# A third kind of expert tile, weight loads moved to ScalarE's queue, and two smaller moves, in a fused sliding-window attention and mixture-of-experts kernel

## The chip, the cores and the metric

The kernel runs on one core of a Trainium2 chip. The metric is the device time of one execution in microseconds. A core has TensorE (PE: matmuls and transposes, with PEld for its weight loads), VectorE (DVE), ScalarE (ACT), GpSimd (POOL) and SyncE (SP, which here only issues transfers). Each takes its own instructions in order. PE writes to PSUM, which has eight banks of 512 float32 values for each of 128 partitions.

## The reference

Attention first: 8 batches, 8 heads, 576 positions, head size 64; each position sees itself and the 63 before it. The result, as 4608 tokens of 512 values, goes through a mixture of experts: eight experts, each token goes to the one with the largest logit, and the expert's output is weighted with that softmax value.

```python
scores = scale * np.matmul(q, k.transpose(0, 1, 3, 2))
rel = pos[:, None] - pos[None, :]
mask = (rel >= 0) & (rel < window)          # window = 64
attn = softmax(where(mask, scores, -1e9))
x = (attn @ v) as (4608, 512)               # tokens
logits = x @ w_gate                         # (4608, 8)
expert_idx = np.argmax(logits, axis=1)
gate_w = softmax(logits)[its own expert]
for e in range(8):                          # the tokens of expert e
    h = np.maximum(x_e @ w1[e], 0.0)        # w1[e]: 512 x 1024
    y_e = h @ w2[e]                         # w2[e]: 1024 x 512
out = gate_w * y
```

All is float32. The experts have no capacity limit: how many tokens an expert gets is known only on the chip.

## The kernel before

**Attention (to about 217 us).** The 16 pairs of (two batches, two heads) are "units"; each unit is done in three steps of three query tiles, 48 steps in all. `step(s)` (line 941) runs several stages of neighbouring steps: q and k are loaded by SP (`load_qk`, line 537; the last 64 positions by `load_rests`, line 548; v by `load_v`, line 561, which POOL then copies into a second alignment), transposed by PE (line 595), multiplied to scores in banks 0 and 1 (line 628), masked by DVE (line 641), exponentiated by ACT (line 651), transposed (line 659), multiplied with v (`weighted`, line 665, always into bank 6), divided by DVE (`divided`, line 680) and turned for the gate's logits. The order of all instructions is written out by hand (`manual_schedule`): each engine gets them as the code calls them. At the start, all loads stand in SP's queue: q and k of unit 0, the rests of batch group 0, v of unit 0, then q and k of unit 1, and so on (lines 921 to 928).

**Routing (about 217 to 250 us).** Tokens are counted per expert (`choose`, line 733), `starts` (line 216) turns counts into numbers of tiles on DVE, and `slot_table` (line 835) makes the list `perm_i` of the token in each slot. The first two tiles, of expert 0, are computed meanwhile.

**Expert tiles (from about 220 us).** A tile has 256 slots. For a *whole* tile `hidden` (line 336) and `output` (line 393) compute each of the two layers by a Strassen-like scheme with seven products instead of eight of half-size blocks. The weights stand in PE in the first layer, and sums of weight blocks are made by POOL beforehand (`sums_w1`, `sums_w2`). The first layer's seven products go to banks 0, 1 and 6 and end in ACT's relu steps; in the second layer DVE makes sums of the hidden blocks first. An expert's *last* tile with at most 160 tokens is a *half* tile (`half_tile`, line 436): 32 matmuls with standing weights and 160 moving columns, then the second layer with the hidden values standing and the weights moving, for tokens 128 to 159 in four column groups of 32 (line 465), and for the first 128 tokens whole (line 470).

Around each tile (`body`, line 479) the work for others is placed: `finish` (DVE) and `scatter` (POOL) write the tile before; `between` lets POOL form the next weights' sums; `turned_blocks` lets DVE turn the next tile's tokens by 16 block transposes (line 315); `keep_turned` (ACT, line 325) copies them to where PE reads, and `sums_x` (DVE) makes the sums; `gather` (POOL) fetches the tokens of the tile after. The weights have two buffers; those of expert e+1 are loaded by SP at the start of expert e (lines 1066 to 1068), when the buffer of e-1 is free.

Which tiles an expert has is decided on the chip: `expert` (line 1063) emits, for each expert and each possible number of tiles up to three, both kinds of tile as separate code, and each engine branches (lines 1076 and 1077) on registers that hold the number of tiles and of whole tiles.

Of the kernel before, what the change touches and what calls it, by code (L numbers as in the profile page):

```python
# [36 lines left out]
def kernel(  # L37
# [34 lines left out]
    NW = 2  # L72
    QD = 32
    HALF = P + QD
    NCUT = NT // P
    assert D == WINDOW and 2 * D == P and NG * P == DM and NB * WINDOW == S
    assert S - SM == WINDOW and KB == NV + 1 and NTB * P == BG * S and B % BG == 0 and NTILE * TB <= 128 * P
# [13 lines left out]
    info_i = consts.tile([P, 2 * E + 1], I32, name="info_i")  # L91
    fulls_i, all_i, most_i = info_i[:, 0:E], info_i[:, E : 2 * E], info_i[:, 2 * E :]

    places_i = consts.tile([P, E + 1], I32, name="places_i")
    perm_e = consts.tile([P, NE * C], I32, name="perm_e")
# [57 lines left out]
    def sums_w2(e):  # L153
        form(right_sums(G, s2s[e % NW], *w2q(e)))

    def load_w1(e):
        return nc.sync.dma_start(out=w1s[e % NW][:], in_=w1v[e])

    def load_w2(e):
        nc.sync.dma_start(out=w2s[e % NW][:], in_=w2v[e])  # L160


    oh_all = consts.tile([P, E, NJ], BF16, name="oh_all")
# [63 lines left out]
    zrow = consts.tile([1, DM], F32, name="zrow")  # L227
    nc.vector.memset(zrow[:], 0.0)
# [39 lines left out]
    def form_all(parts):  # L268
        for _ in parts:
            pass  # L270
# [205 lines left out]
            keep_turned()  # L476
            sums_x([xn[:, c] for c in range(C)])

    def body(e, last, after, full, between=None, next_x=True):
# [6 lines left out]
        if not full:  # L486
            half_tile(e, blocks, after, next_x)
            return
        form_all(hidden(e, blocks))
        parts = output(e, blocks, next_x)  # L490
        next(parts)
        if after is not None:
            gather(perm_i[:, after])
        form_all(parts)

    with tc.manual_schedule(), ExitStack() as held, ExitStack() as brief:
# [40 lines left out]
        def load_qk(u):  # L537
            bg, g = units[u]
            qks[u] = [qk_m(((u % 3 + 2) % 3 * 2 + n) * 1024, BG, NV, 2, D) for n in range(2)]
            for i in range(BG):  # L540
                for t, src in zip(qks[u], (q, k)):
                    for h in range(2):
                        nc.sync.dma_start(
                            out=t[:, i, :, h, :],
                            in_=src[bg * BG + i, 2 * g + h, 0:SM, :].rearrange("(p j) d -> p j d", j=NV),
                        )

        def load_rests(bg):

            at = 6144 + bg % 2 * 2048  # L550
            vr = qk_m(at + 1024, BG, H, D)
            rests[bg] = [qk_m(at, H, D), qk_m(at + 512, H, D), vr]
            for t, src in zip(rests[bg], (q, k)):
                for i in range(BG):
                    nc.sync.dma_start(
                        out=t[i * D : (i + 1) * D], in_=src[bg * BG + i, :, SM:S, :].rearrange("h p d -> p h d")
                    )
            for i in range(BG):
                nc.sync.dma_start(out=vr[D:P, i], in_=v[bg * BG + i, :, SM:S, :].rearrange("h p d -> p h d"))
# [105 lines left out]
        def weighted(s, pTs):  # L665
            u, c = divmod(s, NST)
            bg, g = units[u]
            va, vb = v_ring[u % NVR]
            px = banks[6](0, 2, ST, VW)
            for m in range(ST):  # L670
                for a, (bp, i) in enumerate(blocks_of(c * ST + m)):
                    vt = va[:, bp, i // 2] if i % 2 or i == 0 else vb[:, bp, i // 2 - 1]
                    for h in range(2):
                        nc.tensor.matmul(  # L674
                            px[a * D : (a + 1) * D, h, m, :], lhsT=pTs[h][:, m, a * D : (a + 1) * D],
                            rhs=vt[:, h, :], start=True, stop=True, skip_group_check=True,
                        )
            return px
# [189 lines left out]

        def loads():

            _, n = nc.values_load_multi_w_load_instructions(info_i[0:1, :], min_val=0, max_val=NT // P)
# [4 lines left out]
            return [(n[e], n[E + e], places[e]) for e in range(E)], places[E], n[2 * E]  # L876

        def after(s, routing, bg):

# [174 lines left out]
    with tc.manual_schedule():  # L1054
        load_w1(1)
        load_w2(1)
        def at(n):
            n = nc.s_assert_within(
                n, 0, NTILE - 1, skip_runtime_bounds_check_because="a tile with a token is one of the NTILE"
            )  # L1060
            return lambda ahead: bass.ds((n + ahead) * C, C)

        def expert(e):

            fulls, tiles, first = regs[e]
            if 0 < e < E - 1:
                load_w1(e + 1)
                load_w2(e + 1)

            def one(n, full, between=None):  # L1070
                slots = at(first + n)
                body(e, slots(0), slots(3), full, between)

            def more(n, between=None):

                with tc.If(tiles > n) as some_left:  # L1076
                    with tc.If(fulls > n, preferred_fallthrough_block=False) as full:
                        one(n, True, between)
                        if n + 1 < KT:
                            more(n + 1)  # L1080
                    with full.Else():
                        one(n, False, between)
                if between is not None:
                    with some_left.Else():
                        between()

            if e:
                one(0, True, partial(sums_w2, e))
            more(1 if e else NE, partial(sums_w1, e + 1) if e + 1 < E else None)

        def any_number():
# [27 lines left out]
                finish()  # L1119
                scatter(perm_i[:, slots(1)])  # L1120

        with tc.If(most < KT + 1) as few:  # L1122
            for e in range(E):
                expert(e)
            finish()
# [33 lines left out]
```

## Time and profile before

| | us |
|---|---|
| median of 3 runs | 714.86 (714.1 to 715.29) |
| profiled execution | 717.81 |
| its span, first to last instruction | 716.0 |
| PE busy | 688.8 (96%) |
| DVE, ACT, POOL busy | 505.5, 259.4, 356.6 |
| granted clock of PE, mean | 0.994 |
| a whole tile (484.40 to 509.00) | 24.6 |
| a half tile (509.00 to 526.70) | 17.7 |

Durations below come from the profiled execution; times are counted from its first instruction. A row of the timeline is start, duration, engine, line of the code, operation, what it writes from what it reads, partitions x elements, how many in a row, and in brackets how long the engine had been idle and what ended that. A row of the waits is who waited for whom, microseconds in all, how often, and the longest. A row of a line's instructions has the least, median and largest duration in ns. PEldq is PE's sequencer, which handles branches and semaphores ahead of the array. PE's durations overlap, so the spacing of starts is what counts.

### The profile page before, as it was taken

What the parts mean: (1) busy time and instruction counts of PE and PEld (TensorE: products, weight loads), DVE (VectorE), ACT (ScalarE), POOL (GpSimd) and SP (SyncE); (2) the same over time, 40 slices, a digit from 0 to 9 for tenths busy, and PEclk for the clock granted to TensorE, in tenths of its full rate; (3) what the DMA queues carried; (4) which work ended last, traced back from release to release, by engine and by line L of the source; (5) the groups of instructions that cost most, each with busy time, mean ns of one, the idle gap of its engine ahead of it and who ended that gap; (6) DMA issues with size and microseconds to landing.
All of it is one profiled execution on the core that took longest, in us unless ns stands there. A gap on an engine that the chain in (4) does not pass through costs nothing. (4 is left out here: it accounts for less than half of the span.)

```text
span 716.0 us, 17981 instructions
## 1 busy us (share of the span) xinstructions
PE 688.8 (96%) x6882; PEld 606.6 (85%) x6882; DVE 505.5 (71%) x1656; ACT 259.4 (36%) x655; POOL 356.6 (50%) x368
## 2 busy tenths in 40 slices
PE   5999999999879999999999999999999999999996
PEld 4787888878768898797999999899979799979995
DVE  3666898898965858685866676586667586667764
ACT  4787888888844211121211121121111121011211
POOL 6113748569375025947562257356264756264022
PEclk9999999999989999999999999999999999999999
DMA  9998889988251382715311531351181531111011
GB/s 165 206 200 184 183 179 229 211 197 235 97 187 38 126 294 66 275 63 190 107 48 61 150 143 61 118 203 37 60 275 60 173 116 57 60 38 45 17 61 58
DMA packets 137143, 94.42 MB, mean 132 GB/s; under 512 B 116591, under 2 KB 116607, under 8 KB 137024
## 3 DMA queue, kind: packets, MB, share of 16 engines
q1 hardware_dynamic: 127328, 62.14, 33.0%
q0 software_dynamic: 9120, 28.60, 12.4%
q10 hardware_dynamic: 576, 2.10, 0.9%
q8 instruction: 74, 1.21, 0.7%
q14 instruction: 45, 0.37, 0.2%
HBM read 73.94 MB, written 20.45 MB: 132 GB/s over the span
## 5 line engine op out<-in xcount | busy, mean ns | idle before, releaser
L315 DVE STREAM_TRANSPOSE v_m<-qk_m 32x256 f32<-32x256 f32 x320 | 139.2, 435 | 8.4 <-DMA qk_m<-x_dram,at_g 2.4
L275 POOL DMA_INDIRECT qk_m<-x_dram,at_g x42 | 45.4, 1081 | 174.8 <-DVE v_m L315 145.8
L344 PE MATMUL bank<-qk_m,s 128*128 128x128 f32 x1024 | 122.5, 275 | 0.4 <-DVE qk_m L365 0.4
L344 PEld LDWEIGHTS bank<-qk_m,s 128*128 128x128 f32 x1024 | 118.3, 192 | 0.6 <-issue 0.6
L651 ACT ACTIVATE pr<-pr,mx 128x128 f32<-128x128 f32 x288 | 89.7, 391 | 33.8 <-DVE mx L641 32.1
L344 PE MATMUL bank<-qk_m,w 128*128 128x128 f32 x768 | 93.9, 275 | 0.8 <-PEq L1076 0.8
L344 PEld LDWEIGHTS bank<-qk_m,w 128*128 128x128 f32 x768 | 90.6, 192 | 4.3 <-issue 3.9
L641 DVE CUSTOM_DVE_ANT_0 pr<-bank,mask 128x128 f32<-128x128 f32 x288 | 64.4, 286 | 29.4 <-PE bank L628 28.0
L384 DVE TENSOR_TENSOR v_m<-bank,v_m 128x256 f32<-128x256 f32 (+1 forms) x95 | 43.8, 480 | 40.9 <-PE bank L388 25.9
L295 POOL DMA_INDIRECT out_dram<-v_m,at_s x42 | 42.6, 1013 | 54.0 <-DVE v_m L384 49.9
L569 POOL COPY v_m<-v_m 64x520 f32<-64x520 f32 x32 | 19.8, 618 | 69.4 <-DMA v_m<-in_v_dram 63.3
L140 POOL TENSOR_TENSOR s<-w 128x1024 f32<-128x1024 f32 x22 | 52.2, 2371 | 0.0
L674 PEld LDWEIGHTS bank<-v_m,pT 128*64 128x64 f32 x1152 | 40.6, 139 | 11.0 <-DVE xs L688 4.9
L674 PE MATMUL bank<-v_m,pT 128*64 128x65 f32 x1152 | 47.3, 229 | 2.2 <-DVE xs L688 2.1
L351 ACT COPY qk_m<-bank 128x512 f32<-128x512 f32 x16 | 9.4, 586 | 108.5 <-PE bank L344 70.3
L388 PE MATMUL bank<-qkT_m,v_m 128*128 128x256 f32 x216 | 48.3, 379 | 0.0
L628 PE MATMUL bank<-qkT_m 64*64 64x128 f32 x1152 | 45.9, 289 | 0.1
L595 PE MATMUL bank<-ident,qk_m 128*128 128x128 f32 x256 | 37.0, 287 | 9.4 <-DMA qk_m<-in_q_dram 7.4
L388 PEld LDWEIGHTS bank<-qkT_m,v_m 128*128 128x128 f32 x216 | 41.0, 190 | 5.5
L327 ACT COPY qk_m<-v_m 128x512 f32<-128x512 f32 x40 | 22.7, 615 | 62.4 <-DVE v_m L315 62.4
L444 PEld LDWEIGHTS bank<-qk_m,w 128*128 128x128 f32 x320 | 43.9, 190 | 0.9 <-issue 0.7
L444 PE MATMUL bank<-qk_m,w 128*128 128x160 f32 x320 | 44.4, 299 | 0.4 <-ACT qk_m L327 0.4
(176 smaller groups left out, 1255.4 us busy)
## 6 DMA issues: line engine op xcount, KB each, us to landing
w<-in_moe_w_dram SPq DMA_DIRECT2D x11, 2048.0 KB, 10.0
qk_m<-in_q_dram SPq DMA_DIRECT2D x72, 128.0 KB, 3.7
qk_m<-in_k_dram SPq DMA_DIRECT2D x72, 128.0 KB, 3.8
v_m<-in_v_dram SPq DMA_DIRECT2D x64, 128.0 KB, 3.9
qk_m<-in_moe_w_dram SPq DMA_DIRECT2D x3, 2048.0 KB, 11.1
x_dram<-xs POOLq DMA_DIRECT2D x6, 512.0 KB
x_dram<-xs POOLq DMA_DIRECT2D x3, 768.0 KB
w<-in_moe_w_dram ACTq DMA_DIRECT2D x4, 512.0 KB, 5.8
```

The lines of the kernel that those rows point to most:

```text
L140: op()
L275: G.indirect_dma_start(out=xg[c], out_offset=None, in_=x_dram[:, :], in_offset=bass.IndirectOffsetOnAxis(ap=at_g[:, c : c + 1], axis=0),)
L295: put = G.indirect_dma_start(out=out[:, :], out_offset=bass.IndirectOffsetOnAxis(ap=at_s[:, c : c + 1], axis=0), in_=ys[c], in_offset=None ...
L315: V.transpose(out=xn[b * QD : (b + 1) * QD, :, :, a * QD : (a + 1) * QD].rearrange("p c g i -> p (c g) i"), in_=rows[a * QD : (a + 1) * QD ...
L344: nc.tensor.matmul(acc[:, f, :], lhsT=a[:, g, f * P : (f + 1) * P], rhs=b[:, g, :], start=(first and f == 0 and g == 0), stop=(g == HG - 1 ...
L384: plus = lambda out, a, b: V.tensor_tensor(out=out, in0=a, in1=b, op=ALU.add)
L388: nc.tensor.matmul(acc, lhsT=a[:, f, :], rhs=b[:, f, :], start=(start and f == 0), stop=(stop and f == HF - 1), skip_group_check=True,)
L444: nc.tensor.matmul(acc[:, i], lhsT=w1[:, g, f * P : (f + 1) * P], rhs=xq[:, g].rearrange("p c s -> p (c s)")[:, 0:HALF], start=(i + g == 0 ...
L628: nc.tensor.matmul(out_, lhsT=qT[rows, t, a * WINDOW : (a + 1) * WINDOW], rhs=rhs, start=True, stop=True, skip_group_check=True,)
L641: V.tensor_tensor_reduce(out=prs[h][:, m, :], in0=scs[h][:, m, :], in1=mask[:, m0 + m, :], scale=-scale, scalar=-2 * MASKED, op0=ALU.add, ...
L651: nc.scalar.activation(out=y, in_=y, func=AF.Exp, scale=-1.0, bias=mx[:, h, m : m + 1])
L674: nc.tensor.matmul(px[a * D : (a + 1) * D, h, m, :], lhsT=pTs[h][:, m, a * D : (a + 1) * D], rhs=vt[:, h, :], start=True, stop=True, skip_ ...
```

## The change

1. *A third kind of tile.* A last tile with at most 96 tokens is a *rest* tile (`rest_tile`): in both layers the tokens stand and the weights move. Tokens 64 to 95 use four column groups of 32, tokens 0 to 63 two groups of 64. The hidden values then have tokens on the partitions, so PE transposes them before the second layer. `starts` now makes one number for each expert, the sum of three counts of tiles, with limits of 0, 96 and 160 tokens for the last tile, and the branches compare it with 3n, 3n+2 and 3n+1.
2. *The next expert's weights* are issued on ACT's queue in the expert's first tile, after the third and the fifth of the seven first-layer products, not by SP at the start of the expert.
3. *The last two steps' values* (`weighted`) go to banks 0 and 1, not to bank 6.
4. *The first k* (unit 0's, and the rest of batch group 0) are issued by ACT, and q and k of unit 1 stand before v of unit 0.

```diff
+    REST = P - QD
-    fulls_i, all_i, most_i = info_i[:, 0:E], info_i[:, E : 2 * E], info_i[:, 2 * E :]
+    kinds_i, most_i = info_i[:, 0:E], info_i[:, E:]
+    parts_i = consts.tile([P, 2, E], I32, name="parts_i")
-    def load_w1(e):
-        return nc.sync.dma_start(out=w1s[e % NW][:], in_=w1v[e])
+    def load_w1(e, queue=nc.sync):
+        queue.dma_start(out=w1s[e % NW][:], in_=w1v[e])
...
     def starts():
-        for got, slots in ((fulls_i, TB - 1 - HALF), (all_i, TB - 1)):
-            V.tensor_scalar(out=got, in0=count[:], scalar1=float(slots), scalar2=float(TB), op0=ALU.add, op1=ALU.max)
+        def tiles_over(got, rest):
+            V.tensor_scalar(
+                out=got, in0=count[:], scalar1=float(TB - 1 - rest), scalar2=float(TB), op0=ALU.add, op1=ALU.max
+            )
             V.tensor_single_scalar(got, got, TB.bit_length() - 1, op=ALU.arith_shift_right)
-        V.tensor_copy(out=nt[:], in_=all_i)
-        V.tensor_reduce(out=most_i, in_=nt[:], axis=AX.X, op=ALU.max)
+        tiles_over(kinds_i, 0)
+        V.tensor_copy(out=nt[:], in_=kinds_i)
...
+        for n, rest in enumerate((REST, HALF)):
+            tiles_over(parts_i[:, n], rest)
+            V.tensor_tensor(out=kinds_i, in0=kinds_i, in1=parts_i[:, n], op=ALU.add)
+        V.tensor_copy(out=e_m[:], in_=kinds_i)
+        V.tensor_reduce(out=most_i, in_=e_m[:], axis=AX.X, op=ALU.max)
...
+    L = P // 2
+    hr, hr4 = qk_m(8192, FF // 2), qk_m(8192 + FF // 2, FF // 4)
+    ht, ht4 = qk_m(8960, HF, 2, L), qk_m(8960 + HF * P, HF // 2, 4, QD)
+    def rest_tile(e, blocks, after, next_x):
+        w1, w2 = w1s[e % NW], w2s[e % NW]
+        def rows(acc, tokens, ways):
+            n, width = P // ways, FF // ways
+            for g in range(NG):
+                for c in range(ways):
+                    nc.tensor.matmul(
+                        acc[c * n : (c + 1) * n, 0:width], lhsT=xq[:, g, 0, tokens],
+                        rhs=w1[:, g, c * width : (c + 1) * width], start=(g == 0), stop=(g == NG - 1),
+                        skip_group_check=True,
+                    )
+        a, b = banks[0](0, FF // 2), banks[1](0, FF // 4)
+        rows(b, slice(L, L + QD), 4)
+        relu(out=hr4, in_=b)
+        rows(a, slice(0, L), 2)
+        relu(out=hr, in_=a)
+        for h, t, acc in ((hr4, ht4, banks[3](0, HF // 2, P)), (hr, ht, banks[6](0, HF, P))):
+            for i in range(h.shape[1] // P):
+                nc.tensor.transpose(out=acc[:, i], in_=h[:, i * P : (i + 1) * P], identity=ident[:])
+            nc.scalar.copy(out=t.rearrange("p i c s -> p i (c s)"), in_=acc)
+        V.memset(v1, 0.0)
+        V.memset(yw2, 0.0)
+        form_all(blocks)
+        if after is not None:
+            gather(perm_i[:, after])
+        y, y4 = banks[7](0, DM), y2(0, P)
+        for f in range(FT):
+            for c in range(4):
+                nc.tensor.matmul(
+                    y4[c * QD : (c + 1) * QD], lhsT=ht4[:, f % (HF // 2), f // (HF // 2)],
+                    rhs=w2[:, f, c * P : (c + 1) * P], start=(f == 0), stop=(f == FT - 1), skip_group_check=True,
+                )
+        for f in range(FT):
+            for c in range(2):
+                nc.tensor.matmul(
+                    y[c * L : (c + 1) * L, c * HM : (c + 1) * HM], lhsT=ht[:, f % HF, f // HF],
+                    rhs=w2[:, f, c * HM : (c + 1) * HM], start=(f == 0), stop=(f == FT - 1), skip_group_check=True,
+                )
+        for c in range(4):
+            nc.scalar.copy(out=yps[0][L : L + QD, c * P : (c + 1) * P], in_=y4[c * QD : (c + 1) * QD])
+        if next_x:
+            keep_turned()
+            sums_x([xn[:, c] for c in range(C)])
+        nc.scalar.copy(out=yps[0][0:L, hi_], in_=y[L:, hi_])
+        V.tensor_copy(out=yps[0][0:L, lo_], in_=y[0:L, lo_])
...
-        form_all(hidden(e, blocks))
+        for n, _ in enumerate(hidden(e, blocks), 1):
+            if n in loads:
+                loads[n]()
...
-                for t, src in zip(qks[u], (q, k)):
+                for t, src, queue in zip(qks[u], (q, k), (nc.sync, nc.sync if u else nc.scalar)):
...
-            px = banks[6](0, 2, ST, VW)
+            px = banks[6 if s < N - 2 else s - N + 2](0, 2, ST, VW)
...
+        load_qk(1)
         load_v(0)
-        load_qk(1)
...
             if 0 < e < E - 1:
-                load_w1(e + 1)
-                load_w2(e + 1)
+                loads = {3: partial(load_w1, e + 1, nc.scalar), 5: partial(load_w2, e + 1, nc.scalar)}
...
-                with tc.If(tiles > n) as some_left:
-                    with tc.If(fulls > n, preferred_fallthrough_block=False) as full:
-                        one(n, True, between)
+                with tc.If(kind > 3 * n) as some_left:
+                    with tc.If(kind > 3 * n + 2, preferred_fallthrough_block=False) as full:
+                        one(n, whole_tile, between)
                         if n + 1 < KT:
                             more(n + 1)
                     with full.Else():
-                        one(n, False, between)
+                        with tc.If(kind > 3 * n + 1) as half:
+                            one(n, half_tile, between)
+                        with half.Else():
+                            one(n, rest_tile, between)
```

More of the change, by code (lines that the diff above doesn't have):

```diff
@@ L90 @@
     perm_i = consts.tile([P, NS], I32, name="perm_i")
-    info_i = consts.tile([P, 2 * E + 1], I32, name="info_i")
-    fulls_i, all_i, most_i = info_i[:, 0:E], info_i[:, E : 2 * E], info_i[:, 2 * E :]
+    info_i = consts.tile([P, E + 1], I32, name="info_i")
+    kinds_i, most_i = info_i[:, 0:E], info_i[:, E:]
+    parts_i = consts.tile([P, 2, E], I32, name="parts_i")
     places_i = consts.tile([P, E + 1], I32, name="places_i")
@@ L154, in sums_w2, with load_w2 @@
         form(right_sums(G, s2s[e % NW], *w2q(e)))
-    def load_w1(e):
-        return nc.sync.dma_start(out=w1s[e % NW][:], in_=w1v[e])
-    def load_w2(e):
-        nc.sync.dma_start(out=w2s[e % NW][:], in_=w2v[e])
+    def load_w1(e, queue=nc.sync):
+        queue.dma_start(out=w1s[e % NW][:], in_=w1v[e])
+    def load_w2(e, queue=nc.sync):
+        queue.dma_start(out=w2s[e % NW][:], in_=w2v[e])
     oh_all = consts.tile([P, E, NJ], BF16, name="oh_all")
@@ L477, in half_tile @@
             sums_x([xn[:, c] for c in range(C)])
-    def body(e, last, after, full, between=None, next_x=True):
+    L = P // 2
[46 more added lines that the diff above has]
+        V.tensor_copy(out=yps[0][0:L, lo_], in_=y[0:L, lo_])
@@ L481, in body, with whole_tile @@
+    def whole_tile():
+        pass
+    def body(e, last, after, tile_, between=None, next_x=True, loads=()):
         finish()
@@ L485, in body @@
         blocks = turned_blocks() if next_x else iter(())
-        if not full:
-            half_tile(e, blocks, after, next_x)
+        if tile_ is not whole_tile:
+            tile_(e, blocks, after, next_x)
             return
-        form_all(hidden(e, blocks))
+        for n, _ in enumerate(hidden(e, blocks), 1):
+            if n in loads:
+                loads[n]()
         parts = output(e, blocks, next_x)
@@ L540, in load_qk @@
             for i in range(BG):
-                for t, src in zip(qks[u], (q, k)):
+                for t, src, queue in zip(qks[u], (q, k), (nc.sync, nc.sync if u else nc.scalar)):
                     for h in range(2):
-                        nc.sync.dma_start(
+                        queue.dma_start(
                             out=t[:, i, :, h, :],
@@ L552, in load_rests @@
             rests[bg] = [qk_m(at, H, D), qk_m(at + 512, H, D), vr]
-            for t, src in zip(rests[bg], (q, k)):
+            for t, src, queue in zip(rests[bg], (q, k), (nc.sync, nc.sync if bg else nc.scalar)):
                 for i in range(BG):
-                    nc.sync.dma_start(
+                    queue.dma_start(
                         out=t[i * D : (i + 1) * D], in_=src[bg * BG + i, :, SM:S, :].rearrange("h p d -> p h d")
@@ L869, in loads @@
         def loads():
-            _, n = nc.values_load_multi_w_load_instructions(info_i[0:1, :], min_val=0, max_val=NT // P)
+            _, n = nc.values_load_multi_w_load_instructions(info_i[0:1, :], min_val=0, max_val=3 * NT // P)
             _, places = nc.values_load_multi_w_load_instructions(
@@ L875, in loads @@
             )
-            return [(n[e], n[E + e], places[e]) for e in range(E)], places[E], n[2 * E]
+            return list(zip(n[0:E], places[0:E])), places[E], n[E]
         def after(s, routing, bg):
@@ L1063, in expert, with one @@
         def expert(e):
-            fulls, tiles, first = regs[e]
+            kind, first = regs[e]
+            loads = {}
             if 0 < e < E - 1:
-                load_w1(e + 1)
-                load_w2(e + 1)
-            def one(n, full, between=None):
+                loads = {3: partial(load_w1, e + 1, nc.scalar), 5: partial(load_w2, e + 1, nc.scalar)}
+            def one(n, tile_, between=None):
                 slots = at(first + n)
-                body(e, slots(0), slots(3), full, between)
+                body(e, slots(0), slots(3), tile_, between, loads=() if n else loads)
             def more(n, between=None):
-                with tc.If(tiles > n) as some_left:
-                    with tc.If(fulls > n, preferred_fallthrough_block=False) as full:
-                        one(n, True, between)
+                with tc.If(kind > 3 * n) as some_left:
+                    with tc.If(kind > 3 * n + 2, preferred_fallthrough_block=False) as full:
+                        one(n, whole_tile, between)
                         if n + 1 < KT:
@@ L1087, in expert @@
             if e:
-                one(0, True, partial(sums_w2, e))
+                one(0, whole_tile, partial(sums_w2, e))
             more(1 if e else NE, partial(sums_w1, e + 1) if e + 1 < E else None)
@@ L1120, in any_number @@
                 scatter(perm_i[:, slots(1)])
-        with tc.If(most < KT + 1) as few:
+        with tc.If(most < 3 * KT + 1) as few:
             for e in range(E):
```

## The prediction

> **What bounds the kernel now.** I read the page's busy shares first, then who TensorE (PE) waited for, then the two kinds of expert tile in order of time, and last PE's branches.
>
> ```profile
> PE 688.8 (96%) x6882; PEld 606.6 (85%) x6882; DVE 505.5 (71%) x1656; ACT 259.4 (36%) x655; POOL 356.6 (50%) x368
> ```
> ```profile
> PE bank L595 <- DMA qk_m<-in_q_dram: 7.4, 4, 4.7
> PE bank L699 <- DVE pT L661: 3.1, 4, 1.4
> PE bank L914 <- DVE hi_e L907: 2.7, 1, 2.7
> PE bank L674 <- DVE xs L688: 2.1, 4, 0.9
> PE bank L595 <- DMA qk_m<-in_k_dram: 1.8, 4, 0.7
> PE bank L344 <- PEq L1076: 0.8, 1, 0.8
> PE bank L344 <- DVE qk_m L365: 0.4, 1, 0.4
> ```
> ```profile
> 509.05 8.86 PE L444 MATMUL bank<-qk_m,w 128*128 128x160 f32 x64
> 517.83 1.96 PE L465 MATMUL bank<-qk_m 128*32 128x128 f32 x64
> 519.72 7.13 PE L470 MATMUL bank<-qk_m 128*128 128x512 f32 x16
> 526.69 0.50 PE L344 MATMUL bank<-qk_m,w 128*128 128x128 f32 x3
> ```
> ```profile
> 457.11 1.89 PE L388 MATMUL bank<-w,v_m 128*128 128x256 f32 x8
> 459.79 2.02 PE L344 MATMUL bank<-qk_m,w 128*128 128x128 f32 x16 [0.78 <-PEq L1076]
> ```
> ```profile
> L1077 PEldq COMPARE_BRANCH  x19: 67/342/6568, 270.9 to 705.7; - x19
> ...
> L1076 PEldq COMPARE_BRANCH  x2: 190/2218/4245, 455.0 to 459.4; - x2
> ```
> PE is busy 96% and its waits sum to some 21 us, most of them before 20 us and between 200 and 220 us. The expert stage is a line of tiles without gaps: a whole tile takes 24.6 us (484.45 to 509.05), a half tile 17.65 us (509.05 to 526.69), whatever VectorE (DVE) and ScalarE (ACT) do beside it. So a microsecond taken from or added to PE in this stage moves the end by as much. The last two fences show the only thing that stopped PE between tiles: a branch that took 4245 ns instead of the usual 68 to 342.
>
> **Part 1, the rest tile.** From the inputs I worked out the routing: 669, 400, 748, 505, 592, 390, 566, 738 tokens. Expert 0's count stays over 512. The last tiles hold 157, 144, 236, 249, 80, 134, 54 and 226 tokens, so five are half tiles now (L444: 320 records, 64 a tile) and two of them, of experts 4 and 6, become rest tiles. A float32 matmul shows as two records. Start to start, a record costs 111.6 ns for 128 moving columns, 138 ns for 160 (8.78/64), 216 for 256 and 436 for 512 (6.97/16), and 29.5 ns for 128 columns in four 32-wide column groups (1.89/64), a quarter. The rest tile issues:
> - 32 tokens, four groups, 256 columns: 32 records at 216/3.8 = 57 ns: 1.8 us.
> - 64 tokens, two groups, 512 columns: 16 at 436/2: 3.5 us. No row has exactly two groups; the nearest is L674 (64-wide outputs, 65 columns), 24 records in 0.90 us = 37 ns, against some 59 for one alone by the same slope. I take 2 and bound it by 1.
> - 6 transposes, 12 records at 110 to 128 ns (L306): 1.4 us. Those of the second half wait for the relu of 512 columns (0.6 us, L454) that starts as PE ends the 512-column products; the first half's four records hide 0.5 us of it: gap 0.45.
> - second layer: 64 records at 29.5 = 1.9 us, and 32 of 256 columns in two groups at 108 = 3.5 us.
>
> The sum is 12.5 us, against 17.65: -5.15 a tile, -10.3 in all. DVE must do finish, two memsets and 16 block transposes (16 x 0.44) first, about 8.5 us from the tile's start, then ACT's four small copies and keep_turned end near 11.6: under PE's 12.5, cover 0.9 us. The gather leaves at 8.5 and is read some 4 us into the next, whole, tile.
>
> [...] The rest tile changes mode more often than the half tile. The row: L444 to L465 to L470 passes with starts 8.78 and 1.89 us apart and no gap that the trace shows, so I charge nothing; at 0.2 us (estimate: the pipeline tail, 1.96-1.89 and 7.13-6.97) for four more changes it would be 0.8 us a tile, kept for the range.
>
> **Part 2, the branches, which speak against it.** In the program each level has half, full (next level inside), rest, in this order; rest lies behind full. In instructions (four a float32 matmul): half 291, full 337, rest 314. [...] the instruction queue has 74 packets, 1.21 MB, 16.4 KB each; PE's jumps over one half tile took 342 to 348 ns, except 3805 where two block bounds lay between; over 632 instructions 4245; over 960, 6568 and 6132. The 3805 showed as no wait, the two 6 us ones neither, because PE had the 16 long L470 matmuls (7 us) queued. Behind a whole tile the queue holds about 18 records of 216 ns, 3.9 us; behind a rest tile 18 of 108 ns, 1.95 us. I took the block bounds from the jumps of before, and laid the new program on them:
> - expert 2's last full tile must now jump over 632 instructions (before: none): +0.3. Expert 3's second tile now crosses two bounds: +0.3.
> - end of expert 3: the 4.25 us fetch is there already (0.78 exposed), but it lands in a stub behind which another jump follows at once, into a block whose fetch has only begun. In the trace the next fetch starts 0.7 us after the jump, takes 1.0 and is usable 1.4 later: 3.1 us. So 4.25+3.1+0.3-3.9 = 3.7 exposed: +2.9.
> - start of both rest tiles: behind half and full, 628 instructions, a fetch each: +0.5 each. End of expert 4's rest tile: two bounds, 4.1-1.95: +2.2. End of expert 6's: one bound, its block fetched: 0.
> - ends of the halves of experts 0, 1, 5: fetches under the 7 us: 0. Expert 7: +0.1 on a doubtful bound.
>
> Sum +6.8. By the branch row alone[...] (342 ns, hidden by the queue), it would be 0. I take the sum[...].
>
> **Part 3, first k by ScalarE.** SP issues a q or k load of 128 KB in 0.65 us, so its first 26 end at 18.4 us. Six go to ACT, whose six issues (3.9 us) and table load (1.28) end at 6.0, while its first copy is due at about 6.5: covered by 0.5 us. All that SP issues comes 3.9 us sooner, less 2.6 for v(0), which queues behind unit 1's eight (5.2 us): v(0) is issued from 11.2 instead of 10.3 and used at 21.2 before. Early packets arrive at 200 GB/s, SP's pace, and later stretches reach 240, so two queues gain a little: first q and k both at 5.5 (q was at 4.7, k at 6.1), second pair at 7.7. The first scores start at 9.7, not 10.46: -0.75. Then the waits for q at 17.69 (1.07) and at 55.48 and 56.63 (1.13, 0.53) should shrink, as SP issued without a pause from 34 to 75 us and is now 3.9 ahead. All would be -3.5; I take -2.5, since other waits can move up; from 0 to -4.
>
> **Part 4, banks, weights, counts.** The last two values got their own banks: the waits of 0.50 at 213.04 and 0.89 at 216.38 for DVE's division go, but pT's copies end only 0.6 before the second: -1.1. Products x and y take banks 0 and 1 later than their divisions end.
> The next weights leave SP (issued at 284.36 and 292.97, across a gather) for ACT, after the third and fifth product: 0.37 us each, ahead of relu steps with 1.1 us of idle time, so hidden; without cover 0.7 us a tile on the second layer's operands. 4 MB at some 250 GB/s land by 24 us of the tile; POOL's sums need w1 at 25. Gain: the 0.45 wait at 304.05 (L365): -0.45.
> starts() has 14 instead of 9 small DVE operations, at 0.16: 0.8 us, in a stretch (226 to 245) where DVE is full and PE already waits for hi (0.3 at 241.95): +0.8. The 17 registers become 9: nothing that the trace shows.
>
> **Sum.** -10.3 + 6.8 - 2.5 - 1.1 - 0.45 + 0.8 = -6.75. The profiled execution took 717.81 (span 716.0), 2.95 over the median of 714.86; no term depends on that, so 717.81-6.75 is 711.06 as a profiled time and 714.86-6.75 = 708.1 as a median.
>
> **Rivals.**
> - *Fetches cost nothing* [...]: 714.86-10.3-2.5-1.1-0.45+0.8 = 701.3. For it: of PE's six branches of 2.9 us or more, one shows as a wait. Against: that one, 0.78 at 459.79.
> - *The start gives nothing*, as 16 DMA engines are already busy (share 1.00 from 6 to 12 us): 710.6. For it: DMA reads 9 in the slices up to 150 us.
> - *Pairs of 64-wide groups do not overlap*: rows() of 64 tokens and its second layer cost 7.0 instead of 3.5 us each, +7.0 a tile: 708.1+14.0 = 722, slower. It decides from an overlap of 1.35 down, where 3.4 a tile use up the 6.75. Against: 37 ns at L674.
> - *No tile takes the new path*: then -10.3 and +2.2+1.0 of it go, 715.2: ruled out as far as the counts above are right.
>
> **How the numbers follow.** Case one (708.1, own range 704.5 to 711.5) 0.55; fetches free 0.2; start without gain 0.17; pairs 0.05; no new path 0.03. A measurement of this kernel tells about 0.2% (1.4 us) from no change. Slower than 716.3: pairs, and a little of the last, 0.06; within 0.2%: 0.04; faster 0.9. The range reaches to the free fetches, 701, and up to 712.5, where the start gains nothing and mode changes cost 0.8 a tile.
>
> **What would show it.** Right: two rest tiles of about 12.5 us, each behind a gap of about 0.5 us put down to PE's queue; a gap of about 2 us at expert 4's end and 3.5 at expert 3's; first scores before 10 us; no wait at L674's last two groups; 1 us of wait for hi. Wrong: those gaps missing (then near 701), or 64-token groups with over 300 ns a record at 512 columns.

## The result and the profile after

The changed kernel takes **707.78 us** (median of 4 runs, 706.77 to 708.33), the kernel before took 715.08 on the same chip (4 runs, 714.1 to 716.48): a ratio of 0.9884, 95% interval 0.9861 to 0.9906, so 7.3 us less. The profiled execution of after took 708.33 with a span of 706.5; that of before 717.81 and 716.0, which is 2.7 above the median of its kernel. The spans therefore differ by 9.5, and it is these 9.5 that the rows below add up to. The forecast of 708.1 was met, in part by luck: two terms of it, the branches and the start, were wrong in opposite directions.

The busy shares, and who TensorE (PE) waited for in the whole span:

```profile
PE 678.2 (96%) x6894; PEld 594.9 (84%) x6894; DVE 502.8 (71%) x1657; ACT 262.4 (37%) x665; POOL 356.4 (50%) x368
```
```profile
PE bank L664 <- DMA qk_m<-in_q_dram: 6.8, 2, 6.2
PE bank L354 <- issue: 6.2, 4, 3.1
PE bank L983 <- DVE hi_e L976: 2.7, 1, 2.7
PE bank L768 <- DVE pT L730: 1.4, 1, 1.4
...
PE bank L514 <- ACT qk_m L511: 0.7, 2, 0.3
PE bank L501 <- issue: 0.7, 2, 0.3
PE bank L398 <- ACT v_m L412: 0.5, 1, 0.5
```

(Columns: total us, number of waits, longest. L664 is before's L595, L354 its L344, L398 its L388, L983 its L914.) The waits for k are gone and those for q are the first load and one more. One of the signs named ahead fails in this execution: its first scores start at 10.62, not before 10 us (10.46 in before); in the five variants of the changed kernel below that keep its start and its buffers, they start between 9.0 and 9.6. New is 6.2 us in which PE, at the first layer of a whole tile, "waits for issue", that is, for nothing but its own instructions. The 0.45 for the operands of a new expert (L365 before) is gone; there is one new wait of 0.5 for ScalarE in the first tile.

The timeline of PE around expert 4's rest tile (start, us, engine, line, shape, records, and in brackets the idle time ahead):

```profile
509.07 5.52 PE L501 MATMUL bank<-w,qk_m 128*32 128x256 f32 x48 [0.32 <-issue]
514.52 0.44 PE L514 MATMUL bank<-ident,qk_m 128*128 128x128 f32 x2
515.28 0.66 PE L514 MATMUL bank<-ident,qk_m 128*128 128x128 f32 x4 [0.33 <-ACT qk_m L511]
515.87 1.96 PE L525 MATMUL bank<-qk_m 128*32 128x128 f32 x64
517.75 3.67 PE L531 MATMUL bank<-qk_m 128*64 128x256 f32 x32
521.36 0.82 PE L354 MATMUL bank<-qk_m,w 128*128 128x128 f32 x5
```

509.07 to 521.36 is 12.29 us; the other rest tile, 613.38 to 625.67, takes the same. The only idle time inside is the 0.33 ahead of the second transposes.

The end of expert 3, after its last whole tile:

```profile
449.49 1.89 PE L398 MATMUL bank<-w,v_m 128*128 128x256 f32 x8
454.50 0.46 PE L354 MATMUL bank<-qk_m,w 128*128 128x128 f32 x2 [3.13 <-issue]
457.54 3.15 PE L354 MATMUL bank<-qk_m,w 128*128 128x128 f32 x14 [2.58 <-issue]
460.48 2.65 PE L354 MATMUL bank<-qk_m,s 128*128 128x128 f32 x16
462.97 1.95 PE L354 MATMUL bank<-qk_m,w 128*128 128x128 f32 x16
```
```profile
L1146 PEldq COMPARE_BRANCH  x2: 2767/3360/3952, 447.3 to 451.6; - x2
L1146 PEldq EVENT_SEMAPHORE  x1: 51/51/51, 451.4 to 451.4; - x1
```

This is the largest surprise of the profile. PE stops for 3.13 us, issues two records, stops for 2.58 again, and then runs at half speed: 16 records of L354 take 2.65 us in place of 1.95. The clock's record agrees: half rate is granted from 455.1 for 6.8 us. Before, the end of the last whole tile (459.01) to the end of the next expert's first one (484.45) took 25.4 us; now (451.38 to 483.99) it takes 32.6. The second fence shows PE's sequencer there (shortest, median and longest duration in ns, first and last start): a jump of 3952 ns from 447.3, one of 2767 from 451.6, and between them, at 451.4, an instruction on a semaphore. That instruction turns out to matter.

### The profile page after: what moved, and what is told of

Read it like the earlier page. It is cut to its first block, busy times and chain, and to the rows that moved or that the text cites. A ratio compares the mean times of both kernels' runs of the same rounds, so it can differ in the third digit from the quotient of the medians.

```text
span 706.5 us, 18016 instructions
## 1 busy us (share of the span) xinstructions
PE 678.2 (96%) x6894; PEld 594.9 (84%) x6894; DVE 502.8 (71%) x1657; ACT 262.4 (37%) x665; POOL 356.4 (50%) x368
## 3 DMA queue, kind: packets, MB, share of 16 engines
q0 software_dynamic: 9120, 28.60, 12.4%
## 5 line engine op out<-in xcount | busy, mean ns | idle before, releaser
L354 PE MATMUL bank<-qk_m,s 128*128 128x128 f32 x1024 | 123.2, 276 | 0.0
L354 PEld LDWEIGHTS bank<-qk_m,s 128*128 128x128 f32 x1024 | 119.1, 193 | 0.5 <-issue 0.5
L354 PE MATMUL bank<-qk_m,w 128*128 128x128 f32 x768 | 95.8, 278 | 6.2 <-issue 6.2
L354 PEld LDWEIGHTS bank<-qk_m,w 128*128 128x128 f32 x768 | 91.8, 194 | 9.4 <-issue 9.0
L743 PEld LDWEIGHTS bank<-v_m,pT 128*64 128x64 f32 x1152 | 40.6, 139 | 10.2 <-issue 4.3
L398 PE MATMUL bank<-qkT_m,v_m 128*128 128x256 f32 x216 | 48.3, 379 | 0.0
L364 DVE TENSOR_TENSOR qk_m<-bank,qk_m 128x512 f32<-128x512 f32 x16 | 11.1, 691 | 48.6 <-PE bank L354 48.6
L398 PEld LDWEIGHTS bank<-qkT_m,v_m 128*128 128x128 f32 x216 | 41.0, 190 | 5.5
L728 PE MATMUL bank<-ident,pr 128*128 128x128 f32 x288 | 43.3, 288 | 0.0
L664 PE MATMUL bank<-ident,qk_m 128*128 128x128 f32 x256 | 35.8, 286 | 6.8 <-DMA qk_m<-in_q_dram 6.8
## 6 DMA issues: line engine op xcount, KB each, us to landing
qk_m<-in_moe_w_dram ACTq DMA_DIRECT2D x3, 2048.0 KB, 10.2
```

What stands on the lines that cost most here:

```text
L354: nc.tensor.matmul(acc[:, f, :], lhsT=a[:, g, f * P : (f + 1) * P], rhs=b[:, g, :], start=(first and f == 0 and g == 0), stop=(g == HG - 1 ...
L398: nc.tensor.matmul(acc, lhsT=a[:, f, :], rhs=b[:, f, :], start=(start and f == 0), stop=(stop and f == HF - 1), skip_group_check=True,)
L728: nc.tensor.transpose(out=tr[:, m, :], in_=prs[h][:, m, :], identity=ident[:])
L743: nc.tensor.matmul(px[a * D : (a + 1) * D, h, m, :], lhsT=pTs[h][:, m, a * D : (a + 1) * D], rhs=vt[:, h, :], start=True, stop=True, skip_ ...
```

## The experiments

Each ratio is to the kernel before, run beside it on the same chip; the chips differ, so that before's median was 716.3 to 716.8 in these. Against it, the changed kernel's 0.9884 would be 708.0 to 708.5.

### Where PE's code lies: two dead paddings

PE's code is fetched in pieces. In before's trace, from the transfer that starts at 20.24 us up to the one at 217.82, a stretch in which PE takes no branch, there are 26 transfers of 16 KB on an instruction queue (q8) and 6629 records of PE's instructions: 255 for each transfer. The layouts here take blocks of 256 instructions, which agrees with this count.

```
             with half.Else():
                 one(n, rest_tile, between)
+                if e == 0:
+                    for i in range(51):
+                        nc.tensor.matmul(yps[0], lhsT=hp[:, i % FT, 0:P], rhs=w2s[0][:, i % FT, :], ...)
```

(30 in the second kernel.)

> The changed kernel with 51 more float32 matmuls (204 instructions) at the end of expert 0's rest tile, which never runs, since expert 0 ends in a half tile: nothing that is executed changes, but all PE code behind it moves by 204 of 256 instructions. Theory A ([...] the second gap of 2.58 us at 457.54 is there because the last jump of expert 3 lands 8 instructions before a block bound): the landing moves back to 59 instructions before a bound, so the second gap is gone, the first one (3.13) stays, and no other gap grows; the clock falls to half as before and now lies over 6.8 us of work in place of 4.2, so about 1.3 of the 2.6 us are won: 706.5. Theory B (the two jumps in a row, or the clock, make the gaps, wherever the code lies): both gaps as before, 707.8.

> The same with 30 dead matmules (120 instructions). Theory A: the second gap at expert 3's end goes here too, but other jumps now meet the bounds badly: expert 4's rest tile ends with a jump over two bounds, gap of 2.0; expert 6's rest tile starts 5 instructions before a bound, a gap of 2.8 within its first matmuls, after which the clock may fall to half; expert 2's second tile takes a fetch of 4 us and shows 0.2 to 0.3. Sum of gaps 9.0 against 6.4 in the changed kernel: 710.5, and up to 712.5 with half clock. Theory B: as the changed kernel, 707.8, gaps in the same places.

Measured: with 51 matmuls **706.27 us, ratio 0.9845** (0.9813 to 0.9877), span 704.7; with 30 **716.17 us, ratio 0.9994** (0.9976 to 1.0011), span 713.6. The same instructions are executed in both. PE's timeline with 51 at expert 3's end:

```profile
450.34 1.89 PE L398 MATMUL bank<-w,v_m 128*128 128x256 f32 x8
455.92 3.75 PE L354 MATMUL bank<-qk_m,w 128*128 128x128 f32 x16 [3.69 <-issue]
459.46 3.01 PE L354 MATMUL bank<-qk_m,s 128*128 128x128 f32 x16
```

One gap in place of two, as theory A said, though the one that stays grew from 3.13 to 3.69. From the end of expert 3's last tile to the end of expert 4's first one it is 31.1 us in place of 32.6, so 1.5 are won where 1.3 were expected; the ratios of this kernel and of the changed one are not clear of each other (their intervals overlap). With 30, at expert 2's end, expert 3's end, the end of expert 4's rest tile and the start of expert 6's:

```profile
403.67 2.02 PE L354 MATMUL bank<-qk_m,w 128*128 128x128 f32 x16 [0.43 <-issue]
...
407.30 1.27 PE L354 MATMUL bank<-qk_m,s 128*128 128x128 f32 x10 [0.93 <-issue]
...
457.87 3.44 PE L354 MATMUL bank<-qk_m,w 128*128 128x128 f32 x16 [3.68 <-issue]
...
523.46 2.02 PE L354 MATMUL bank<-qk_m,w 128*128 128x128 f32 x16 [1.56 <-DVE v_m L394]
...
618.38 2.15 PE L501 MATMUL bank<-w,qk_m 128*32 128x256 f32 x20 [2.32 <-issue]
```

The gaps stand where the bounds were expected to put them: 1.56 (2.0 expected), 2.32 (2.8), 0.43 and 0.93 (0.2 to 0.3 expected, so 1.1 too little). The total was underrated, 716.2 against 710.5 to 712.5. Part of the rest is the clock: half rate also from 618.7 for 3.4 us, so that with its gap this rest tile took 16.85 us in place of 12.29. Another 1.4 lies behind the last tile, where PE's last jump took 4907 ns against 2924 with 51. Theory B falls: nothing but the place of the code was changed, and some 10 us hang on it.

### One long jump in place of two

```
-with tc.If(kind > 3 * n) as some_left:
+with tc.If(kind > 3 * n, preferred_fallthrough_block=False) as some_left:
```

(with the 51 dead matmuls).

> As with 51 dead matmuls, and the branch that asks whether a level has any tile has its empty side put first (fallthrough), so that an expert that has ended takes one long jump, not a jump to a stub and a second jump. Theory A: at expert 3's end one fetch of 4.0 us behind the whole tile's 3.9 us of queued matmuls: gap of 0.2 to 0.5 in place of 3.13 and 2.58, no half clock; the start of the rest tiles, now two taken branches, 0.7 us in place of 0.3. From the middle of expert 3's last tile to the end of expert 4's first one 25.8 us in place of 32.8: 707.8 - 7.0 + 0.7 = 701.5. Theory B, if the gap comes from the length of the jump: 3 us or more still there, about 705.

Measured: **708.21 us, ratio 0.9877** (0.9846 to 0.9908): no gain over the padding alone; this execution also reached its first expert tile 3.6 us later than that one. From the end of expert 3's last tile to the end of expert 4's first one it is 31.2 us, as with the padding alone (31.1). At expert 3's end, the timeline and the sequencer:

```profile
460.01 3.75 PE L354 MATMUL bank<-qk_m,w 128*128 128x128 f32 x16 [3.96 <-issue]
```
```profile
L1146 PEldq COMPARE_BRANCH  x2: 69/1834/3599, 452.0 to 456.2; - x2
L1146 PEldq EVENT_SEMAPHORE  x1: 51/51/51, 456.1 to 456.1; - x1
```

One jump, as meant, but it begins at 456.2, when PE's last matmul has ended (456.05), and not some 4 us earlier, as the jumps behind this tile in before (455.0, with the last matmul ending at 459.01) and in the changed kernel (447.3 and 451.38). Both theories missed. In the program the empty side of that branch holds one instruction for PE ahead of the jump: it waits until PE's own semaphore has reached the count of all matmuls so far, and adds the counts of the tiles that are left out. In these traces it stands at the end of the last matmul (456.1 here, 451.4 in the changed kernel), and the jump from the empty side begins behind it, covered by nothing. In before it was there too, but the jump behind it was short: 190 ns, 0.78 us of gap in all.

```profile
L1076 PEldq EVENT_SEMAPHORE  x1: 51/51/51, 459.3 to 459.3; - x1
```

### The empty side without the wait

```
 with tc.If(kind > 3 * n, preferred_fallthrough_block=False) as some_left:
     ...
-if between is not None:
-    with some_left.Else():
-        between()
+with some_left.Else():
+    if between is not None:
+        between()
+    nc.tensor.matmul(tps[1][0:1, 0, 0:1], lhsT=ident[:, 0:1], rhs=ident[:, 0:1], start=True, stop=True, ...)
```

(and 43 dead matmuls). With a matmul on the empty side, the counts ride on that matmul.

> The changed kernel with three edits to code that does no work of the tiles: the empty side of the branch on a level comes first in the program, so that an expert that has ended makes one jump; that side issues one matmul of one column into a free bank, on which the count of PE's semaphore rides, so that PE need not wait for its own last matmul before it jumps (with the empty side first but without this, the one jump of 3599 ns began only at 456.25, 0.19 us after the last matmul had been finished, and cost 3.96); 43 dead matmuls put the block bounds where no landing lies close before one. Theory A (the wait for its own semaphore takes away the cover of 3.9 us of queued matmuls): at expert 3's end 0.1 to 0.5 us of gap in place of 3.13 and 2.58, full clock after it; rest tile starts up to 0.8 each; gaps and half clock sum to 2.5 where the changed kernel has 8.8: about 6.5 us faster than it, 701. Theory B (the wait is for something else, such as the length of the jump): 3.5 to 4 us of gap remain, about 704 to 706.

Measured: **703.25 us, ratio 0.98** (0.9763 to 0.9837), the fastest kernel of the study: some 5 to 6 us under the changed kernel, where theory A had expected 6.5. The timeline and the sequencer at expert 3's end, and the start of the next rest tile:

```profile
452.10 1.89 PE L398 MATMUL bank<-w,v_m 128*128 128x256 f32 x8
453.92 0.19 PE L1165 MATMUL bank<-ident 128*1 128x1 f32 x2
454.54 2.02 PE L354 MATMUL bank<-qk_m,w 128*128 128x128 f32 x16 [0.43 <-issue]
456.40 1.95 PE L354 MATMUL bank<-qk_m,s 128*128 128x128 f32 x16
...
504.68 5.52 PE L501 MATMUL bank<-w,qk_m 128*32 128x256 f32 x48 [0.71 <-issue]
```
```profile
L1146 PEldq COMPARE_BRANCH  x2: 69/2024/3979, 450.0 to 450.4; - x2
```

A jump of the same length, 3979 ns, now begins at 450.4, 3.6 us before the last matmul of the tile ends, and 0.43 us of it is seen. From here to the end of the last tile the clock stays full. From the end of that tile to the end of expert 4's first one it is 25.2 us (453.99 to 479.21) in place of 32.6. Theory A holds: against the kernel with the single jump and the wait (and 8 dead matmuls more), 5.5 us are won.

### Without the rest tile, in the same layout

```
-for n, rest in enumerate((REST, HALF)):
+for n, rest in enumerate((0, HALF)):
```

> The changed kernel whose counts never ask for the rest tile (the bound for it set to 0 tokens), so that experts 4 and 6 end in half tiles; the code lies where it lay. Theory: each of the two tiles costs 5.36 us more, the gaps at rest tile starts and at expert 6's end (0.32, 0.34, 0.29) go, and the stall at expert 3's end stays as it is: 707.8 + 10.7 - 0.95 = 717.5, slower than the kernel before (715.1), because the layout costs 7.3 and the rest of the change gives less than 8. Rival: the rest tile earns less than its span says, since waits move (the gather, the operands of the next tile): under 714.

Measured: **719.42 us, ratio 1.0057** (1.0034 to 1.0079), slower than the kernel before. The half tile of expert 4 runs from 510.07 to 527.71, 17.64 us; the rest tile with the gap ahead of it took 12.61. Twice 5.0, less the 0.3 at expert 6's end, is the 9.8 that was expected. The ratio shows 12.4 (some 2 either way); in this execution expert 3's end also cost more (gaps of 3.75 and 2.97 us, 1.0 more in sum, and half clock for 10.2 us in place of 6.8, part of it inside the gaps): 34.6 us from the end of its last tile to the end of expert 4's first one, in place of 32.6, which is 2.0 of it. Without its rest tile the change would be a loss: its branches cost more than its other edits earn.

### The start's edits, in the kernel before

```
-for t, src in zip(qks[u], (q, k)):
+for t, src, queue in zip(qks[u], (q, k), (nc.sync, nc.sync if u else nc.scalar)):
...
-load_v(0)
 load_qk(1)
+load_v(0)
```

Both edits (with the same one for the first rests), the queue alone, and the order alone:

> The kernel before with the start of the change alone: first k (unit 0 and the first rest) issued by ScalarE, unit 1's q and k ahead of v(0). Theory A (the whole difference of 6.7 us at the start of the slot matmuls is made by these two edits): 6 to 7 us faster than before, ratio 0.991. Theory B (the 2.5 us of the prediction come from them, the rest from elsewhere in the change or from the clock that was granted in the first 25 us): ratio 0.9965.

> The kernel before with first k by ScalarE alone, v(0) still ahead of unit 1. Theory A: SP's queue is 3.9 us ahead for all later loads, so the waits at 55.48 and 56.63 (1.66) and the one at 17.69 (1.07) go, and those for pT with them: 4 to 5.5 us faster. Rival: what was won was the order, and this gives 1 to 2 us.

> The kernel before with unit 1's q and k ahead of v(0) alone. Theory A: the wait for unit 1's q at 17.69 (1.07) goes, since those loads are issued 2.6 us sooner, and v(0), 5.2 us later, is still in time for 21.2; the waits at 55 us stay, since from unit 2 on SP is where it was: 1 to 1.5 us faster. Rival: the whole gain comes from the order: over 4.

Measured: both **716.72 us, ratio 0.9995** (0.9979 to 1.0011); the queue **716.22, 0.9985** (0.9971 to 0.9999); the order **718.53, 1.0017** (1.0002 to 1.0031). No theory A holds, nor does theory B. The queue alone gains 1.1 us, in the range of its rival, but the order, to which that rival gives the gain, is 1.2 slower. Together, the edits that I had made responsible for the start gain nothing that can be measured in the kernel before. Yet the slot matmuls (L983, L914 before) begin at 205.5 in before and at 198.75 in after, and in all executions of the changed kernel and its variants so far between 198.0 and 203.7, while these three stand at 203.1, 205.5 and 206.4. Something else in the change moves the start. The single executions spread by several us, so these starts are no more than a sign. The loads' rows gave another: from issue to landing k takes 3.4 us in after, 3.8 in before, and 4.0 to 4.1 in these three.

What else differs is where the buffers lie. The change shrinks one small table and adds another, parts_i, so that everything allocated behind them stands 32 bytes higher in SBUF: the buffer of q and k begins at 73984, a multiple of 256, where it began at 73952, 224 over. (That of v moves from 133344 to 133376, but its rows of 256 bytes stand 260 apart, so most of them are off in either case.)

### Thirty-two bytes

```
+spare = consts.tile([P, 8], I32, name="spare")
 places_i = consts.tile([P, E + 1], I32, name="places_i")
```

> The kernel before with nothing but 32 unused bytes a partition set ahead of the table places_i, so that q's, k's and v's buffers begin at SBUF addresses 73984 and 133376, which 64 divides, as in the changed kernel (whose new table parts_i moved them), where before they begin at 73952 and 133344 (32 over). Theory C (the 256-byte packets of q, k and v are slower into addresses that are 32 over: 19.1 to 19.6 ns each from 20 to 150 us and 23 to 29 in the first 15 us in the kernel before and its three variants, 18.1 and 18 to 20 in all six executions of the changed kernel and its variants): packets of 18.1, first 16 transposes done 2 to 4 us sooner, slot matmuls before 203, and 3 to 5 us less in all: ratio 0.994. Theory A (the start's edits are what gains): no difference.

> The same 32 bytes and the start of the change (first k by ScalarE, unit 1 ahead of v(0)) in the kernel before. Theory C with no part for the start's edits: as with the 32 bytes alone, ratio 0.994. Theory D (the edits gain only when the packets are quick, since otherwise both queues wait for the same 16 DMA engines): 2 to 3 us more than the 32 bytes alone, ratio 0.990 to 0.991, slot matmuls at 199 to 201.

> The changed kernel with 32 unused bytes a partition ahead of places_i, so that q's, k's and v's buffers are 32 bytes over a multiple of 64 again (74016, 133408); nothing else. Theory C: packets of 19 ns and more, slot matmuls at 203 to 205, 3 to 5 us slower than the changed kernel: about 712, ratio to the kernel before 0.994 to 0.996. Rival: the changed kernel's own time, ratio 0.988.

Measured: before with 32 bytes **714.5 us, ratio 0.9971** (0.9951 to 0.9991); with 32 bytes and the start's edits **711.73, ratio 0.9908** (0.9876 to 0.994); the changed kernel moved off again **713.37, ratio 0.9941** (0.9917 to 0.9965), against its own 0.9884. Slot matmuls begin at 202.0, 199.2 and 202.75. The loads' rows (queue, number, size, us from issue to landing) in the changed kernel, and in the one moved off:

```profile
qk_m<-in_q_dram SPq DMA_DIRECT2D x72, 128.0 KB, 3.6
qk_m<-in_k_dram SPq DMA_DIRECT2D x66, 128.0 KB, 3.4
v_m<-in_v_dram SPq DMA_DIRECT2D x64, 128.0 KB, 3.2
```
```profile
qk_m<-in_q_dram SPq DMA_DIRECT2D x72, 128.0 KB, 4.1
qk_m<-in_k_dram SPq DMA_DIRECT2D x66, 128.0 KB, 4.0
v_m<-in_v_dram SPq DMA_DIRECT2D x64, 128.0 KB, 4.1
```

Averages over the 256-byte packets in the traces say it more sharply (how many started from 4 to 15 us, their mean time, and the mean from 20 to 150 us):

```
buffers            start's edits      packets 4-15   ns 4-15   ns 20-150   us (ratio)
224 over 256       no   (before)          7977         23.3       19.3     1
224 over 256       the order alone        7760         23.7       19.6     1.0017
224 over 256       the queue alone        7688         28.6       19.1     0.9985
224 over 256       yes                    7672         27.8       19.4     0.9995
multiple of 256    no                     8654         19.2       18.1     0.9971
multiple of 256    yes                    9661         20.0       18.2     0.9908
changed kernel, multiple of 256           9236         20.0       18.1     0.9884
changed kernel, 32 over 256               8180         28.6       19.3     0.9941
```

Theory D's numbers are the ones that hold; theory C had the packets right, but alone the 32 bytes gain 2.1 us, not 3 to 5. With a second queue in the first 15 us, each packet slows by 4 to 5 ns where the destinations are off, and fewer packets get through than with one queue; where they are aligned, it slows by 0.8 and 12% more get through. So the two parts gain 2.1 us and nothing apart (ratios 0.9971 and 0.9995, which would make 0.9966), and 6.6 together (0.9908, interval 0.9876 to 0.994). Why a packet into an address that is off slows when a second queue is added was not tested.

## Why the prediction was right, and where it was not

**The rest tile** (predicted 12.5 us, -10.3 for two). Right: 12.29 each, -10.7. The largest unknown, two 64-wide column groups side by side, was taken at 218 ns a record for 512 columns and measured 228 (the group L501, 128x512: 7.3 us over 32 records of two tiles). The rival of pairs that don't overlap is out. The changes between 32-wide, 64-wide and whole column groups show no gap (the only idle time inside the tile is the 0.33), so the charge of nothing was right by the row. Each transpose is one record, not two, and their gap was 0.33, not 0.45.

**The branches** (predicted +6.8). The layout of the code in blocks of 256 instructions was the right one to follow, and the rival that fetches are free is out: two paddings of dead code, of 204 and 120 instructions, moved the gaps to where the layout puts them. (Which blocks are already there when PE jumps was assumed; no run measured it by itself.) But two terms failed, and a third held better than it looks.
- *The instruction count.* "Four a float32 matmul" was applied to the transposes too; they take two (L514 has 12 weight loads and 12 matmul records for the 12 transposes of two tiles). The rest body has 302 instructions, not 314, and the error added up along the experts. With 302, my layout of the code agrees with the trace on which jumps had to be fetched for: expert 3's second tile needs no fetch (+0.3 predicted), expert 4's rest tile ends without a gap (+2.2 predicted), and expert 3's end lands just before a bound, which adds a third fetch (2.58 us, not predicted). The transfers of PE's instructions have it: 16 KB each from 448.77 and 451.96, behind the two jumps, and a third from 455.16 to 456.23, 1.3 us before PE goes on.
- *The two jumps at expert 3's end.* The sum "4.25+3.1+0.3-3.9 = 3.7" came to 3.13, by about the way that it describes: the first jump took 3.95 and was covered (it began 4.0 us before the last matmul ended), the second took 2.77 and was seen whole. The wait for PE's own semaphore is not in the sum, but costs little here, because the first jump ended at 451.30, just before the last matmul (451.38). It decides when there is one jump alone: then it takes away the cover, as the run with one long jump shows. Nor were the 0.78 us in before all due to the jump of 4245 ns: that ended 0.2 us after the last matmul, and the wait and the second jump came behind it.
- *The clock.* No term for it: half rate for 6.8 us after the gaps. The 32 records of the first two products took 5.9 us without the gap inside them, in place of 3.6 in the run without the wait: 2.3 us.

In sum expert 3's end cost 7.2 more than before (32.6 against 25.4), not 2.9: 2.35 for the first gap (3.13 in place of 0.78), 2.58 for the third fetch, 2.3 for the clock; with 0.25 at expert 2's end, 0.66 at two rest tile starts (1.0 predicted) and 0.29 at expert 6's end, the branches came to +8.4.

**The start** (predicted -2.5, up to -4). The mechanism given, SP's pace of issue, is not enough: in the kernel before, the same edits gain nothing that can be measured. The trace shows -6.8 at the slot matmuls, and the ratios show that it takes the edits together with the move of the buffers by 32 bytes, which the prediction did not look at: the new table stood in the diff, and the addresses behind it were not compared. The rival "the start gives nothing, as 16 DMA engines are already busy" described the edits alone correctly. The -6.8 is from one pair of executions; with the five variants that keep the changed kernel's start and buffers, the slot matmuls begin between 198.0 and 203.7. What supports it is the 6.6 by the ratio for the edits and the 32 bytes together.

**Banks** -1.1 predicted; from the first slot matmul to the first product of the hidden layer 13.56 us became 12.56, -1.0 (13.55 to 13.56 in all six executions with the old banks, 11.75 to 12.58 in the seven with the new ones). **starts()**: +0.8 predicted; the same two waits of 0.3 for hi remain and one of 0.5 for ScalarE comes: +0.5. ScalarE had just stood idle for 0.41 for a sum of VectorE (L380) that the longer starts() holds up. **Weights by ScalarE**: -0.45 predicted, the wait is gone. With the old loads it varied, from no wait (the start's edits alone) over 1.1 (the order alone) and 1.2 (the 32 bytes alone) to 1.6 (both); why was not found, since these loads are issued sooner when the start is.

Sum in the profiled executions: -10.7 + 8.4 - 6.8 - 1.0 + 0.5 - 0.45 = -10.05, where the spans differ by 9.5; the 0.55 left over was not traced. So the cost of the branches was underrated by 1.6 and the gain of the start by 4.3. The medians differ by 7.3 and not 9.5, since before's profiled execution lies 2.7 over its median and after's 0.55; it is this 7.3 that lies close to the 6.75 of the forecast.

## What to carry to other kernels

Before a branch is put around large bodies, lay the code out in blocks (here of about 256 instructions), with the instructions of each kind counted from the program and the bounds found from the jumps of an earlier trace, and ask of every taken jump how many bounds it crosses, how close before one it lands (here a gap of 2.3 to 3.0 us came from that), and whether anything makes the engine run dry ahead of it. An empty side of a branch is not free: once the two jumps had been made one, a cheap instruction of the engine that must stay ahead took away a wait that cost 5.5 us with what hung on it. And where a change adds or shrinks any buffer, compare the addresses of all that lie behind it: a move of 32 bytes decided here whether the other edits gained anything.

## What the runs showed of the hardware

- With the buffer of q and k at a multiple of 256, packets of 256 bytes took 18.1 to 18.2 ns on average, and 18 to 20 from 4 to 15 us; 224 or 32 bytes over, 19.1 to 19.6, and 23 to 29. It is the destination that was off, and the loss was 5 to 8% on average and 21 to 43% from 4 to 15 us. Smaller multiples (64 or 128) were not told apart from 256, and whether the other buffers that moved by the 32 bytes matter was not tried either.
- Most of PE's jumps took 0.30 to 0.47 us or 2.8 to 4.9 (6.1 and 6.6 over 960 instructions in before), a few 0.75 to 1.7. Where by the layout a jump landed a few instructions before a bound, a gap of 2.3 to 3.0 us came a few matmuls later (2.58 in the changed kernel, 2.97 without the rest tile, 2.32 with 30 dead matmuls).
- The clock fell to half for 3.4 to 10.2 us after gaps of 2.3 to 4.0 us; this holds in all thirteen executions, before's too, for the 2.7 us ahead of the slot matmuls. Behind the first 28 us no gap up to 1.64 was followed by half rate. The shortest gap that was, of 2.32 us (30 dead matmuls, at 618.38), stood 0.6 us behind one of 0.32. In the first 28 us the clock differed from one execution to the next (first full between 9 and 21 us, in four of them half again for 3.4 to 6.8 us, behind pairs of gaps of 0.6 to 2.1 us), so that one profile says little of a gain of 1 or 2 us at the start.
